# Filling TensorE's idle time with matmuls on zeros, an earlier load, sectioned norm columns and fewer table loads in a planned attention and channel-mix kernel

## The chip, the cores and the metric

The kernel runs on one core of one Trainium2 chip. The metric is the device time of one execution in microseconds (us), given as the median of several runs. "Span" is the time from the first to the last instruction in the trace; the device time is about 2 us longer.

Engines in the profile: PE is TensorE's matmul side, PEld its weight load, DVE is VectorE, ACT is ScalarE, POOL is GpSimd, SP is SyncE. L482 means line 482 of the kernel in question. The change shifts line numbers, so each matmul has a pair of them:

| work on TensorE | before | after |
|---|---|---|
| kv = kᵀv of a batch | L308 | L343 |
| transposes of q | L338 | L373 |
| u = q·kv | L358 | L393 |
| sum of squares for the norm | L383 | L425 |
| 1/rms spread to the rows ("rr") | L407 | L452 |
| w_k, w_r, w_v products of the mix | L482, L505, L524 | L537, L560, L580 |
| matmuls on zeros | none | L609 |

## The reference, cut to what matters

Batch 8, 8 heads, sequence 576, head dimension 64; d_model 512, d_ff 1024.

```python
def _attn_ref(q, k, v, g_norm):
    kv = np.einsum('bhsd,bhse->bhde', k, v)
    out = np.einsum('bhsd,bhde->bhse', q, kv)
    rms = np.sqrt(np.mean(out * out, axis=-1, keepdims=True) + 1e-06)
    return (out / rms * g_norm).astype(np.float32)

def _moe_ref(x, mu_k, mu_r, w_k, w_v, w_r):       # x: heads side by side, (8, 576, 512)
    x_prev = ...                                  # x shifted by one token, zeros first
    xk = mu_k * x + (1.0 - mu_k) * x_prev
    xr = mu_r * x + (1.0 - mu_r) * x_prev
    k = np.maximum(xk @ w_k, 0.0)
    v = k * k @ w_v
    r = 1.0 / (1.0 + np.exp(-(xr @ w_r)))
    return (r * v).astype(np.float32)
```

## The kernel before

The 8 batches of attention feed 9 groups of 512 tokens of the mix. Each group takes 32 w_k matmuls, 16 w_r matmuls and 32 w_v matmuls of 512 columns (in one group the w_k matmuls are 64 of 256 columns). All pieces of work are given to a planner in Python, which puts them in an order for each engine from durations it assumes, while the kernel is built. On the chip each engine then works through its own queue in that order: **a piece that waits holds up every piece behind it.** The timelines below show it: while one product of TensorE waits 6.74 us, nothing that stands behind it runs.

```python
class Planner:
    STAY, SWITCH = 4.0, 0.11        # only TensorE has a cost for changing the kind of work
    ...
    def run(self):
        ...                         # for each engine: of the pieces that can start within
        ...                         # 0.02 us of the earliest, the one with the smallest due
```

A piece names engines with assumed durations, the pieces it depends on, the buffers it uses, and `due`, its priority: the smaller, the sooner. This is how q gets transposed and when kv of a batch may start:

```python
        mm = add({"PE": 0.25 * n}, kv_mm, mode=1, bufs=[pkv, kin, vin, kv], due=due(26),
                 deps=[loaded[(m, b, h)] for m in ("k", "v") for h in (2 * hp0, 2 * (hp0 + n) - 1)])
        ...
        if b >= 2:
            def q_dma(_):
                nc.sync.dma_start_transpose(...)          # by DMA, from SyncE's queue
            m = add({"SP": 0.1}, q_dma, bufs=[qin, qT], due=due(30), deps=[loaded[("q", b, 0)]], land=4.2)
        else:
            for hp in hps:
                ...                                       # six transposes on TensorE, then a copy
```

The norm loads ScalarE's table for ln and exp each time, and works on few rows of many columns for the three small parts of batch 0:

```python
        def st_act(_):
            rows = slice(32 * hp0, 32 * hp0 + 32 * n)
            nc.scalar.preload_act_table_set("natural_log_exp_and_others")
            nc.scalar.activation(out=get(ln)[rows], in_=pst.t[rows, :, 0:HS], func=AF.Ln, bias=eps[rows],
                                 scale=1.0 / HD)
            nc.scalar.activation(out=get(rs)[rows], in_=ln.t[rows], func=AF.Exp, scale=-0.5)
```

The PSUM tiles "mm" (the mix) and "at" (attention) are rings of two each.

## Time and profile before

| | before |
|---|---|
| device time, median of 3 | 247.25 us (246.87 to 248.08) |
| span of the profiled run | 244.7 us |
| TensorE busy | 82% |
| first mix matmul | 24.3 us |
| end of TensorE's work | 240.4 us |

How to read it: the page's second part gives the busy share in tenths in 40 equal slices (6.1 us each), the row PEclk gives TensorE's granted clock in tenths of full speed, and the fourth part is the chain of work that ended last, followed back from the end. From the page of the kernel before:

```profile
PE 201.5 (82%) x1442; PEld 94.7 (39%) x1442; DVE 150.5 (62%) x273; ACT 114.4 (47%) x144; POOL 25.2 (10%) x39
...
PE   0564798961681997997999999799999999999981
...
PEclk9999999995586799999999999999999999999998
...
PE 54%; ACT 17%; DMA 17%; DVE 7%; issue 2%; POOL 1%; DVEq 0%; ACTq 0%; POOLq 0%
PE mm L524 22%; PE mm L482 17%; DMA qT<-q 14%; PE mm L505 9%; ACT L388 4%; ACT relu L486 3%; DMA v<-in_v_dram 3%; ACT ln L389 2%; DVE out L528 2%; ACT kv L184 2%; PE at L407 2%; ACT sig L509 2%; PE at L358 2%; ACT L509 2%; ACT rs L391 1%
```

The chain does not go to TensorE alone: the transposes of q by DMA hold 14% of the span. The PE row shows the hole, four slices at 1, 6, 8 and 1 tenths (55 to 80 us), where the clock is down as well (5, 5, 8 and 6). The busy time of the engines in a stretch (start:end and length; then busy time and instructions of PE, PEld, DVE, ACT and POOL; granted clock; DMA share; GB/s) of the kernel before:

```profile
55.00:81.00 26.00, 12.12 (x105) 5.25 (x101) 11.50 (x22) 9.39 (x14) 3.08 (x4) 0.63 1.17 189
```

In 26 us TensorE was busy for 12 us, at 0.63 of the clock. TensorE's timeline (start, duration, line, tile, count; in brackets the idle time before and what ended it) of the kernel before:

```profile
27.30 4.89 PE L505 MATMUL mm<-w_r,xr 128*128 128x512 bf16 x13 [0.17 <-DVE xr L445]
...
62.91 0.69 PE L358 MATMUL at<-qT,kv 64*64 64x288 bf16 x8 [6.74 <-DMA qT<-q]
...
65.03 3.60 PE L482 MATMUL mm<-xk,w_k 128*128 128x512 bf16 x8
...
78.91 0.46 PE L358 MATMUL at<-qT,kv 64*64 64x288 bf16 x4 [6.29 <-DMA qT<-q]
...
234.87 3.61 PE L524 MATMUL mm<-w_v,sqk 128*128 128x512 bf16 x16 [0.84 <-DVE out L528]
239.32 1.02 PE L524 MATMUL mm<-w_v,sqk 128*128 128x512 bf16 x4 [0.84 <-DVE out L528]
```

Two waits for a transposed q, 6.74 and 6.29 us, and after each a cold restart, which means matmuls at half the clock: after the first, 8 matmuls in 3.60 us are 0.45 us each, while 16 in 3.61 us (the line at 234.87) are 0.22 each; after the second (not shown) 4 take 1.70 us by the chain. The line at 27.30 is cold too (13 in 4.89 us, 0.376 each), though the clock row shows full rate there: the trace's own records of the clock begin only at 31.22 us, with a change to full, and the row has nines for all the time before. SyncE's timeline of the kernel before, one line for each group of issues:

```profile
44.66 7.17 SPq L327 DMA_TRANSPOSE qT<-q  x1
...
63.65 27.04 SPq L327 DMA_TRANSPOSE qT<-q  x3
```

The chain puts 18.2 us from the first issue, at 44.66, to its landing at 62.9, and 15.2 us for the next. Last, ScalarE's timeline of the kernel before at the start, the load and the ln of the second of three rounds of table load, ln and exp:

```profile
18.18 1.28 ACT L388 ACT_TABLE_LOAD   x1
19.48 0.73 ACT L389 ACTIVATE ln<-at,eps 32x576 f32<-32x576 f32 x1
```

### The profile page before, as it was taken

Reading aid. Unit: us, or ns where it says so; the run is one execution under the profiler, and the core shown is the slowest. Engines: PE = TensorE matmul, PEld = TensorE weight load, DVE = VectorE, ACT = ScalarE, POOL = GpSimd, SP = SyncE. Lnnn points to the kernel's source line nnn. Section 1 sums busy time; section 2 is a strip of 40 time slices with the busy share of each in tenths; the row PEclk is TensorE's granted clock in tenths of the full one; section 3 lists DMA queues with packets and bytes.
Section 4 is the critical chain, followed back from the end, with each engine's and each line's share of the span. In section 5 each row is a group of like instructions: output and inputs, shape, how many; then the busy total and the mean of one; then the engine's idle time right before and its main releaser. Section 6 shows DMA issues by size and latency. Waiting matters only on the chain.

```text
span 244.7 us, 3619 instructions
## 1 busy us (share of the span) xinstructions
PE 201.5 (82%) x1442; PEld 94.7 (39%) x1442; DVE 150.5 (62%) x273; ACT 114.4 (47%) x144; POOL 25.2 (10%) x39
## 2 busy tenths in 40 slices
PE   0564798961681997997999999799999999999981
PEld 0431245431230453443444457343444444444430
DVE  2359815857430898997899696589779323324222
ACT  2289257432371298089067426906731522513600
POOL 8860003302100124000000000000000000000000
PEclk9999999995586799999999999999999999999998
DMA  6999999999998969999074032004203205006023
GB/s 84 180 210 207 204 203 204 203 191 164 276 192 127 170 115 160 204 239 235 22 164 107 0 98 76 0 0 120 55 0 102 74 0 165 6 7 167 0 86 86
DMA packets 40832, 29.99 MB, mean 123 GB/s; under 512 B 15720, under 2 KB 35696, under 8 KB 40816
## 3 DMA queue, kind: packets, MB, share of 16 engines
q0 software_dynamic: 21008, 16.78, 44.6%
q1 hardware_dynamic: 19808, 12.99, 23.0%
q8 instruction: 11, 0.18, 0.3%
q14 instruction: 5, 0.04, 0.1%
HBM read 33.56 MB, written 9.44 MB: 176 GB/s over the span
## 4 chain that ended last, share of the span: by engine, by line
PE 54%; ACT 17%; DMA 17%; DVE 7%; issue 2%; POOL 1%; DVEq 0%; ACTq 0%; POOLq 0%
PE mm L524 22%; PE mm L482 17%; DMA qT<-q 14%; PE mm L505 9%; ACT L388 4%; ACT relu L486 3%; DMA v<-in_v_dram 3%; ACT ln L389 2%; DVE out L528 2%; ACT kv L184 2%; PE at L407 2%; ACT sig L509 2%; PE at L358 2%; ACT L509 2%; ACT rs L391 1%
## 5 line engine op out<-in xcount | busy, mean ns | idle before, releaser
L482 PE MATMUL mm<-xk,w_k 128*128 128x512 bf16 (+1 forms) x320 | 69.0, 368 | 0.7 <-ACT relu L486 0.4
L524 PE MATMUL mm<-w_v,sqk 128*128 128x512 bf16 x288 | 65.6, 379 | 3.6 <-DVE out L528 1.7
L486 ACT ACTIVATE relu<-mm 128x1024 bf16<-128x1024 f32 x36 | 36.5, 1021 | 50.6 <-PE mm L482 47.9
L482 PEld LDWEIGHTS <-w_k 128*128 128x128 bf16 x320 | 30.6, 99 | 31.9 <-issue 5.3
L524 PEld LDWEIGHTS <-sqk 128*128 128x128 bf16 x288 | 27.8, 98 | 35.8 <-issue 5.4
L528 DVE TENSOR_TENSOR out<-mm,sig 128x1024 f32<-128x1024 f32 (+1 forms) x20 | 22.3, 1116 | 26.2 <-PE mm L524 19.7
L489 DVE TENSOR_TENSOR sqk<-relu 128x1024 bf16<-128x1024 bf16 x36 | 24.5, 689 | 22.5 <-ACT relu L486 22.4
L505 PE MATMUL mm<-w_r,xr 128*128 128x512 bf16 x144 | 35.8, 400 | 1.4 <-DVE xr L445 1.4
L184 ACT CAST uT<-at 128x576 bf16<-128x576 f32 x18 | 11.2, 639 | 37.4 <-PE at L358 37.4
L414 DVE TENSOR_TENSOR xT<-uT,at 128x576 bf16<-128x576 bf16 (+1 forms) x31 | 21.7, 730 | 8.3 <-PE at L407 8.3
L509 ACT ACTIVATE sig<-mm 128x1024 bf16<-128x1024 f32 x18 | 18.2, 1025 | 10.7 <-PE mm L505 10.4
L505 PEld LDWEIGHTS <-xr 128*128 128x128 bf16 x144 | 14.1, 102 | 20.8 <-DVE xr L445 3.2
L441 DVE TENSOR_SCALAR t<-d,mu_sb 128x576 bf16<-128x576 bf16 x64 | 20.1, 372 | 0.1
L358 PE MATMUL at<-qT,kv 64*64 64x288 bf16 x116 | 8.4, 328 | 13.6 <-DMA qT<-q 13.0
L186 DVE CAST uT<-at 128x576 bf16<-128x576 f32 x11 | 8.3, 755 | 14.4 <-PE at L358 14.4
L367 DVE TENSOR_TENSOR sq<-uT 128x576 bf16<-128x576 bf16 x32 | 13.7, 453 | 4.5 <-ACT uT L184 4.2
L407 PE MATMUL at<-rs,selg 128*128 128x288 bf16 (+2 forms) x60 | 12.6, 306 | 4.8 <-DVE xT L414 1.8
L388 ACT ACT_TABLE_LOAD x10 | 12.8, 1283 | 0.2
L407 PEld LDWEIGHTS <-selg 128*128 128x128 bf16 (+2 forms) x64 | 6.1, 102 | 15.4 <-issue 11.1
L358 PEld LDWEIGHTS <-kv 64*64 64x64 bf16 x128 | 3.4, 111 | 22.3 <-issue 14.4
L247 POOL DMA_DIRECT2D k<-in_k_dram x10 | 7.5, 750 | 43.5 <-PE at L308 42.2
L184 ACT CAST kv<-at 64x256 bf16<-64x256 f32 x22 | 8.1, 368 | 8.3 <-PE at L308 5.1
(49 smaller groups left out, 127.6 us busy)
## 6 DMA issues: line engine op xcount, KB each, us to landing
out_dram<-out SPq DMA_DIRECT2D x24, 192.0 KB
k<-in_k_dram POOLq DMA_DIRECT2D x7, 576.0 KB, 12.4
v<-in_v_dram POOLq DMA_DIRECT2D x7, 576.0 KB, 17.2
q<-in_q_dram POOLq DMA_DIRECT2D x7, 576.0 KB, 17.4
out_dram<-out SPq DMA_DIRECT2D x24, 128.0 KB
out_dram<-out SPq DMA_DIRECT2D x24, 64.0 KB
w_k<-in_moe_w_k_dram POOLq DMA_DIRECT2D x1, 1024.0 KB, 12.6
w_v<-in_moe_w_v_dram POOLq DMA_DIRECT2D x1, 1024.0 KB, 16.7
```

Of the source, the lines that this page charges most:

```text
L184: nc.scalar.copy(out=dst, in_=src)
L388: nc.scalar.preload_act_table_set("natural_log_exp_and_others")
L407: nc.tensor.matmul(get(ps)[:, i, 0:HS], selg[rows, hp1 + i, :], rs.t[rows, half, :], start=True, stop=True)
L414: nc.vector.tensor_mul(out=xT.t[:, hs, xs], in0=get(uT)[:, hs].rearrange("q h i jj p -> q h (i jj p)")[:, :, cs], in1=ps.t[:, 0:step, 0:HS])
L441: nc.vector.tensor_scalar_mul(out=get(t)[:, hp - hp0, :], in0=d.t[:, hp, :], scalar1=mu_sb[:, m + hp:m + hp + 1])
L482: nc.tensor.matmul(get(ps)[:, fc % 2, a0:a1], w_k_sb[:, cc, 128 * fc:128 * fc + 128], xk[:, cc, x0:x0 + a1 - a0], start=(cc == 0), stop=(c ...
L486: nc.scalar.activation(out=get(rt), in_=ps.t, func=AF.Relu)
L489: nc.vector.tensor_mul(out=get(sqk)[:, 2 * f2:2 * f2 + 2, :], in0=rt.t, in1=rt.t)
L505: nc.tensor.matmul(get(ps)[:, ci % 2, :], xr[:, cc, n0:n0 + 128], w_r_sb[:, cc, :], start=(cc == 0), stop=(cc == NHP - 1))
L509: nc.scalar.activation(out=get(sg), in_=ps.t, func=AF.Sigmoid)
L524: nc.tensor.matmul(get(ps)[:, ci % 2, :], sqk.t[:, fc, 128 * ci:128 * ci + 128], w_v_sb[:, fc, :], start=(fc == 0), stop=(fc == NFC - 1))
L528: nc.vector.tensor_mul(out=get(ot)[:, xs, :], in0=ps.t[:, xs, :], in1=sg.t[:, xs, :])
```

## The change

Its announced intent has four parts: idle matmuls on zeros fill TensorE's gaps ahead of the mix, so that its clock is up when the mix starts; batch 1 loads ahead of w_v; the norm's columns are cut into sections that sit on more rows; a table is loaded only when it changes. The diff holds more than that: q of batch 2 is transposed on TensorE too (`b >= 3`), a rule keeps kv and q transposes of a batch behind the norm broadcast of the batch before (`last_rr`), there is a fourth output buffer, rings give any free slot, and ScalarE may scale by mu. The core of it:

```diff
 class Planner:
-    STAY, SWITCH = 4.0, 0.11
+    SWITCH = {"PE": 0.11, "ACT": 1.28}
+    SHUN = {"DVE": 0.5}
+    STAY = {"PE": 4.0, "ACT": 4.0}
 ...
+            if warm and p.eng == "PE":
+                since, until, idle = warm
+                n = int((t - max(free.get("PE", 0.0), since)) / 0.23)
+                if n > 0:
+                    order.append(lambda n=n: idle(n))
+                if p is until:
+                    warm = None
 ...
-        "out": (3, (128, 2, C), FP32),
+        "out": (4, (128, 2, C), FP32),
 ...
+    def ln_table():
+        if table[0] != "ln":
+            nc.scalar.preload_act_table_set("natural_log_exp_and_others")
+            table[0] = "ln"
 ...
-    p_wv = add({"POOL": 0.8}, lambda _: load_w(w_v_sb, moe_w_v), due=-698, land=5.2)
-    for b in range(1, B):
+    for n in ("k", "v", "q"):
+        load(1, n, 0, H, -698)
+    p_wv = add({"POOL": 0.8}, lambda _: load_w(w_v_sb, moe_w_v), due=-697, land=5.2)
+    for b in range(2, B):
 ...
-                 deps=[loaded[...] ...])
+                 deps=[loaded[...] ...] + [last_rr[b - 1]])          # kv; q's transposes likewise
 ...
-        if b >= 2:
+        if b >= 3:
 ...
-            m = add({"SP": 0.1}, q_dma, ..., land=4.2)
+            m = add({"SP": 3.2}, q_dma, ..., land=2.5)
 ...
         def st_act(_):
-            rows = slice(32 * hp0, 32 * hp0 + 32 * n)
-            nc.scalar.preload_act_table_set("natural_log_exp_and_others")
-            nc.scalar.activation(out=get(ln)[rows], in_=pst.t[rows, :, 0:HS], ...)
+            ln_table()
+            nc.scalar.activation(out=get(ln)[:, 0:wide, 0:w], in_=pst.t[:, 0:wide, 0:w], ...)
 ...
-            sc = add({"DVE": 0.25 * n}, ...)
+            sc = add({"DVE": 0.365 * n, "ACT": 0.7 * n}, ...)
 ...
+    def idle(n):
+        for _ in range(n):
+            nc.tensor.matmul(get(warm)[:, 0, :], zeros[:, 0:128], zeros, start=True, stop=True)
```

More of the change, by code (lines that the diff above doesn't have):

```diff
@@ L42, in __init__, with add @@
         self.left = []
-    def add(self, on, fn, deps=(), bufs=(), due=0.0, land=0.0, mode=0):
+    def add(self, on, fn, deps=(), bufs=(), due=0.0, land=0.0, mode=None):
         p = Piece(on, fn, deps, bufs, due, land, mode)
@@ L47, in add, with slots @@
         return p
+    def slots(self, tag):
+        out = []
+        for i, old in enumerate(self.rings[tag]):
+            if old is None:
+                out.append((0.0, i))
+            elif all(u.end is not None for u in old.users):
+                out.append((max(u.end for u in old.users) + 0.15, i))
+        return sorted(out)
     def room(self, bufs):
@@ L55, in room, with run @@
         for tag, bs in want.items():
-            for old in self.rings[tag][:len(bs)]:
-                if old is None:
-                    continue
-                if any(u.end is None for u in old.users):
-                    return None
-                t = max([t] + [u.end + 0.15 for u in old.users])
-        return t
-    def run(self):
-        free, order, dma, mode = {}, [], 0.0, 0
+            free = self.slots(tag)
+            if len(free) < len(bs):
+                return None
+            t = max(t, free[len(bs) - 1][0])
+        return t
+    def run(self, warm=None):
+        free, order, dma, modes = {}, [], 0.0, {"PE": None, "ACT": None}
         while self.left:
@@ L78, in run @@
                         t = max(t, d.end + (self.LAT[d.eng] if d.eng != eng or d.land else 0.0))
-                    ways.append((t + us, t, eng))
+                    ways.append((t + us + self.SHUN.get(eng, 0.0), t, eng))
                 _, t, eng = min(ways)
-                stay = self.STAY if eng == "PE" and p.mode == mode else 0.0
+                stay = self.STAY.get(eng, 0.0) if p.mode == modes.get(eng) else 0.0
                 best.setdefault(eng, []).append((t, p.due - stay, p))
@@ L87, in run @@
             t, _, p, p.eng = min(picks, key=lambda x: x[0])
+            if warm and p.eng == "PE":
[5 more added lines that the diff above has]
+                    warm = None
             p.start, p.end = t, t + p.on[p.eng]
-            if p.eng == "PE":
-                p.end += self.SWITCH * (p.mode != mode)
-                mode = p.mode
+            if p.eng in self.SWITCH and p.mode is not None or p.eng == "PE":
+                p.end += self.SWITCH[p.eng] * (p.mode != modes[p.eng])
+                modes[p.eng] = p.mode
             free[p.eng] = p.end
@@ L104, in run @@
                     b.placed = True
-                    self.rings[b.tag].append(b)
-                    self.rings[b.tag].pop(0)
+                    self.rings[b.tag][self.slots(b.tag)[0][1]] = b
             self.left.remove(p)
@@ L109, in run @@
         for p in order:
-            p.fn(p.eng)
-        return order
+            if isinstance(p, Piece):
+                p.fn(p.eng)
+            else:
+                p()
+        return [p for p in order if isinstance(p, Piece)]
 @with_exitstack
@@ L186, in copy @@
             nc.vector.tensor_copy(out=dst, in_=src)
+    table = [None]
+    def ln_table():
+        if table[0] != "ln":
+            nc.scalar.preload_act_table_set("natural_log_exp_and_others")
+            table[0] = "ln"
     ident = const.tile([128, 128], BF16, name="ident")
@@ L194 @@
     eps = const.tile([128, 1], FP32, name="eps")
+    zeros = const.tile([128, 512], BF16, name="zeros")
     sel2 = const.tile([128, 32], BF16, name="sel2")
@@ L204, in consts_small @@
     def consts_small(_):
+        nc.vector.memset(zeros, 0.0)
         nc.vector.memset(g_st, 0.0)
@@ L217, in consts_small @@
             nc.vector.memset(sel2[64 * e:64 * e + 64, e:e + 1], 1.0)
-        nc.scalar.preload_act_table_set("natural_log_exp_and_others")
+        ln_table()
     def consts_idents(_):
         make_identity(nc, ident)
-    p_mu_ps = Buf("at")
+    p_mu_ps, warm = Buf("at"), Buf("mm")
     def consts_mu(_):
@@ L236, in load_w @@
         nc.gpsimd.dma_start(out=dst, in_=src.rearrange("(c p) n -> p c n", p=128))
-    add({"DVE": 0.6}, consts_small, due=-1000)
+    add({"DVE": 0.9}, consts_small, due=-1000)
     src = {"k": k, "v": v, "q": q}
@@ L272 @@
     x_ready = {}
+    last_rr = {-1: None, 0: None}
     def attention(b, parts):
-        bufs = {t: Buf(t) for t in ("qT", "kv", "uT", "sq", "ln", "rs", "xT", "d")}
+        bufs = {t: Buf(t) for t in ("qT", "kv", "uT", "sq", "xT", "d")}
         x_ready[b] = {"k": [], "r": []}
@@ L291, in attention_part @@
         kin, vin, qin = (kvq[(m, b)] for m in ("k", "v", "q"))
-        kv, qT, uT, sq, ln, rs, xT, d = (bufs[t] for t in ("kv", "qT", "uT", "sq", "ln", "rs", "xT", "d"))
+        kv, qT, uT, sq, xT, d = (bufs[t] for t in ("kv", "qT", "uT", "sq", "xT", "d"))
+        ln, rs = Buf("ln"), Buf("rs")
         def due(x):
@@ L318, in attention_part @@
         mm = add({"PE": 0.25 * n}, kv_mm, mode=1, bufs=[pkv, kin, vin, kv], due=due(26),
-                 deps=[loaded[(m, b, h)] for m in ("k", "v") for h in (2 * hp0, 2 * (hp0 + n) - 1)])
+                 deps=[loaded[(m, b, h)] for m in ("k", "v") for h in (2 * hp0, 2 * (hp0 + n) - 1)] + [last_rr[b - 1]])
         kvs = [add({"DVE": 0.25 + 0.14 * n, "ACT": 0.38 + 0.11 * n}, lambda eng, e=e: kv_copy(eng, e), deps=[mm],
@@ L328, in q_dma @@
                     "q (y p) -> q y p", p=NP), in_=qin.t.rearrange("p h x -> p (h x)"))
-            m = add({"SP": 0.1}, q_dma, bufs=[qin, qT], due=due(30), deps=[loaded[("q", b, 0)]], land=4.2)
+            m = add({"SP": 3.2}, q_dma, bufs=[qin, qT], due=due(30), deps=[loaded[("q", b, 0)]], land=2.5)
             qts = {hp: m for hp in hps}
@@ L345, in attention_part @@
                 m = add({"PE": 0.35}, lambda _, hp=hp, ps=ps: q_tr(_, hp, ps), bufs=[ps, qin, qT], due=due(27),
-                        deps=[p_ident, loaded[("q", b, 2 * hp)], loaded[("q", b, 2 * hp + 1)]])
+                        deps=[p_ident, loaded[("q", b, 2 * hp)], loaded[("q", b, 2 * hp + 1)], last_rr[b - 1]])
                 qts[hp] = add({"ACT": 0.65, "DVE": 0.75}, lambda eng, hp=hp, ps=ps: q_cp(eng, hp, ps), deps=[m],
@@ L375, in attention_part @@
                            due=due(20)))
+        nsec = NHP // n
+        sec = S // nsec
         pst = ps_buf()
+        wide = 2 if sec > 512 else 1
+        w = sec // wide
         def st_mm(_):
-            for half in range(2):
-                for hp in hps:
-                    nc.tensor.matmul(get(pst)[32 * hp:32 * hp + 32, half, 0:HS], sel2,
-                                     sq.t[:, hp, HS * half:HS * half + HS], start=True, stop=True)
+            for x in range(wide):
+                for i, hp in enumerate(hps):
+                    for c in range(nsec):
+                        row = 32 * (i * nsec + c)
+                        nc.tensor.matmul(get(pst)[row:row + 32, x, 0:w], sel2,
+                                         sq.t[:, hp, sec * c + w * x:sec * c + w * x + w], start=True, stop=True)
         def st_act(_):
-            rows = slice(32 * hp0, 32 * hp0 + 32 * n)
-            nc.scalar.preload_act_table_set("natural_log_exp_and_others")
-            nc.scalar.activation(out=get(ln)[rows], in_=pst.t[rows, :, 0:HS], func=AF.Ln, bias=eps[rows],
+            ln_table()
+            nc.scalar.activation(out=get(ln)[:, 0:wide, 0:w], in_=pst.t[:, 0:wide, 0:w], func=AF.Ln, bias=eps,
                                  scale=1.0 / HD)
-            nc.scalar.activation(out=get(rs)[rows], in_=ln.t[rows], func=AF.Exp, scale=-0.5)
+            nc.scalar.activation(out=get(rs)[:, 0:wide, 0:w], in_=ln.t[:, 0:wide, 0:w], func=AF.Exp, scale=-0.5)
         m = add({"PE": 0.3}, st_mm, mode=2, deps=sqs, bufs=[pst, sq, ln, rs], due=due(18))
-        st = add({"ACT": 3.9 if b else 1.35}, st_act, deps=[m], bufs=[pst, ln, rs], due=due(17))
+        st = add({"ACT": 0.42 + 0.0018 * sec}, st_act, deps=[m], bufs=[pst, ln, rs], due=due(17), mode="ln")
         xms = []
@@ L404, in rr_mm @@
                 def rr_mm(_, hp1, half, ps):
-                    rows = slice(32 * hp0, 32 * hp0 + 32 * n)
                     for i in range(step):
-                        nc.tensor.matmul(get(ps)[:, i, 0:HS], selg[rows, hp1 + i, :], rs.t[rows, half, :],
-                                         start=True, stop=True)
+                        c0 = HS * half
+                        while c0 < HS * half + HS:
+                            c, off = divmod(c0, sec)
+                            x, off = divmod(off, w)
+                            cnt = min(HS * half + HS - c0, w - off)
+                            nc.tensor.matmul(get(ps)[:, i, c0 - HS * half:c0 - HS * half + cnt],
+                                             selg[:, (hp1 - hp0 + i) * nsec + c, :], rs.t[:, x, off:off + cnt],
+                                             start=True, stop=True)
+                            c0 += cnt
                 def x_mul(_, hp1, cs, xs, ps):
@@ L418, in attention_part @@
                 ps = ps_buf()
-                m = add({"PE": 0.26}, lambda _, hp1=hp1, half=half, ps=ps: rr_mm(_, hp1, half, ps),
+                m = add({"PE": 0.13 * step}, lambda _, hp1=hp1, half=half, ps=ps: rr_mm(_, hp1, half, ps),
                         deps=[st, p_mu], bufs=[ps, rs, xT], due=due(14))
-                xms.append(add({"DVE": 0.14 + 0.3 * step},
+                xms.append(add({"DVE": 0.15 + 0.3 * step},
                                lambda _, hp1=hp1, cs=cs, xs=xs, ps=ps: x_mul(_, hp1, cs, xs, ps),
                                deps=[m] + [us[hp1 + i] for i in range(step)], bufs=[ps, uT, xT], due=due(13)))
+        last_rr[b] = m
         def diff(eng):
@@ L437, in attention_part, with scale @@
             t = Buf("t")
-            def scale(_, m, t):
+            def scale(eng, m, t):
                 for hp in hps:
-                    nc.vector.tensor_scalar_mul(out=get(t)[:, hp - hp0, :], in0=d.t[:, hp, :],
-                                                scalar1=mu_sb[:, m + hp:m + hp + 1])
+                    dst, by = get(t)[:, hp - hp0, :], mu_sb[:, m + hp:m + hp + 1]
+                    if eng == "DVE":
+                        nc.vector.tensor_scalar_mul(out=dst, in0=d.t[:, hp, :], scalar1=by)
+                    else:
+                        nc.scalar.mul(out=dst, in_=d.t[:, hp, :], mul=by)
             def blend(_, dst, t):
@@ L448, in attention_part @@
             late = due(10 - 4 * pos) + (50 * pos if b == 0 else 0)
-            sc = add({"DVE": 0.25 * n}, lambda _, m=m, t=t: scale(_, m, t), deps=[df, p_mu], bufs=[d, t], due=late)
+            sc = add({"DVE": 0.365 * n, "ACT": 0.7 * n}, lambda eng, m=m, t=t: scale(eng, m, t), deps=[df, p_mu], bufs=[d, t], due=late)
             x_ready[b][key].append(add({"DVE": 0.06 + 0.34 * n}, lambda _, dst=dst, t=t: blend(_, dst, t), deps=[sc],
@@ L466, in store @@
             row += cnt
+    p_first = add({"PE": 0.01}, lambda _: None, deps=x_ready[0]["r"] + [p_wr], bufs=[warm], due=-1)
+    hold = add({"PE": 0.01}, lambda _: None, bufs=[warm], due=-2000)
     def mix(g):
@@ L508, in r_sig @@
         def r_sig(_, ps, sg):
+            table[0] = "sigmoid"
             nc.scalar.activation(out=get(sg), in_=ps.t, func=AF.Sigmoid)
@@ L516, in mix @@
                 ms.append(add({"PE": 0.865}, lambda _, ci=2 * c2 + x, ps=ps: r_mm(_, ci, ps),
-                              deps=ms or need["r"] + [p_wr], bufs=[ps, sg], due=u + x))
+                              deps=ms or need["r"] + [p_first], bufs=[ps, sg], due=u + x))
             sigs.append((sg, add({"ACT": 1.04}, lambda _, ps=ps, sg=sg: r_sig(_, ps, sg), deps=ms[1:], bufs=[ps, sg],
-                                 due=u + 2)))
+                                 due=u + 2, mode="sigmoid")))
         def v_mm(_, ci, part, ps):
@@ L548 @@
         mix(g)
-    plan.run()
+    def idle(n):
+        for _ in range(n):
+            nc.tensor.matmul(get(warm)[:, 0, :], zeros[:, 0:128], zeros, start=True, stop=True)
+    plan.run((1.5, p_first, idle))
 _INS = ['q', 'k', 'v', 'g_norm', 'moe_mu_k', 'moe_mu_r', 'moe_w_k', 'moe_w_v', 'moe_w_r']
```

## The prediction

> **What bounds the kernel now.** The 720 channel-mix matmuls of 512 columns take 6.91 us per 32 in the undisturbed late stretch (timeline), 155 us in all; attention of batches 1 to 7 adds about 3.3 us each on TensorE, with 1.4 us more where q is transposed there: about 181 us together. The mix starts at 24.3 us and TensorE ends at 240.4 us, 216 us. So about 35 us of that phase is not work. By the windows view:
> - 54.8 to 80.7 us: TensorE waits for the DMA transposes of q of batches 2 and 3. The chain of waits gives "DMA qT<-q" 14% of the span (18.2 and 15.2 us). The first was issued at 44.66 us behind queued loads of about 2.9 us each. TensorE then restarts at half clock (0.45 us per matmul instead of 0.216). The Trainium skill, "TensorE: Matmul & The Clock Gate", Part 1, says that an idle window of about 3.4 us halves the clock; the trace agrees (granted 0.50 to 0.59 after 6.7 us idle).
> - At 27.3 us, 13 matmuls take 4.89 us (0.376 each): cold too, about 2 us lost, although the clock row shows full rate.
> - Later iterations lose 1 to 1.5 us each around table loads and sigmoid; the end loses about 2 us to an output tile waiting for its store (three buffers).
>
> **What changes.** 64 zero matmuls go in ahead of the mix; k, v, q of batch 1 load before w_v; batch 2 is also transposed on TensorE, leaving 5 DMA transposes; table loads fall from 17 to 12 (1.28 us each; three of those removed are in the start-up chain); ln/exp of the first parts shrink from 576 columns (0.74 and 0.68 us) to 288 and 144 (I estimate 0.45 and 0.35); half of the mu scalings move to ScalarE (0.64 us each against 0.30 on VectorE); a fourth output buffer.
>
> **Costed on the critical path.**
> 1. Start: the ScalarE chain gets about 5 us shorter, but the zeros are unconditional and stand behind the mu matmul, which ends at 4.85 us: 18 of them at 0.43 us cold reach 11 to 12 us, while batch 0's first kv matmul ran at 7.7 us. I expect the first mix matmul at 27 to 29 us, but warm. Net near 0 to -2 us.
> 2. Batch 2's transpose wait disappears. Batch 3's is issued near 53 us and should land about when needed (wait 0 to 4 us). With the cold clock: -16 us.
> 3. New wait: group 1's w_k matmuls are now ordered ahead of group 0's w_v ones, so TensorE waits for xk of batch 1, behind busy ScalarE and VectorE: about 42 to 51 us, +6 us net.
> 4. Steady iterations: r matmuls, then ln, exp, table load and sigmoid on ScalarE: about 1.5 us of wait each, as before: 0 to +2.
> 5. End: -2 us.
>
> Sum: 181 us of work, start at 28, 18 us of waits, tail 4.3: span about 231, time 2.3 more.
>
> **Prediction: 233 us, 224 to 241 (8 in 10). Faster by over 2%: 0.88; within 2%: 0.09; slower: 0.03.**
>
> **Right or wrong in the profile.** The chain's share of "DMA qT<-q" under 3%; clock row full from 30 us on, or one dip at 42 to 51 us; first real w_r matmul between 27 and 29 us; first w_v matmul after 50 us; no output wait for a store at the end.
>
> **What would make it wrong.** If the zeros don't delay the start (mix by 24 us) and the wait for xk is short: 224. If batch 3's and 4's transposes still land late, or a cold restart follows at 45 us: 240.

## More of the kernel before

The mix, for group g (`slot = 20 * g`); relu is on ScalarE, its square on VectorE, and the first w_v matmul of a group needs all four squares:

```python
            a = add({"ACT": 1.04}, ..k_relu.., deps=ms[1:], bufs=[ps, rt], due=u + 2)
            sqs.append(add({"DVE": 0.7}, ..k_sq.., deps=[a], bufs=[rt, sqk], due=u + 4))
        ...
        for c2 in range(2):
            ps, ot, u = Buf("mm"), Buf("out"), slot + 12 + 4 * c2
            ...                                   # w_v matmuls, deps on sqs
```

## The result, and the profile after

Ratios are the mean time of one kernel's runs over that of the other's runs of the same rounds, so they are not quite the ratio of the medians quoted. Executions over 1.5% slower than the fastest of the same kernel are left out of the means.

| | before | after |
|---|---|---|
| device time, median of 4 | 247.06 us (246.62 to 248.08) | 239.5 us (238.14 to 239.78) |
| ratio to before, 95% interval | | 0.9677 (0.9636 to 0.9718) |
| span of the profiled run | 244.7 us | 236.1 us |
| TensorE busy | 82% | 91% |
| first mix matmul | 24.3 us | 28.05 us |
| end of TensorE's work | 240.4 us | 231.7 us |
| table loads | 17 | 12 |

The kernel is 3.2% faster; 5.7% was predicted. The profiled run of after is the fastest of its runs, the others have spans of 237.1 to 237.8 us. From the page of after:

```profile
PE 214.8 (91%) x1538; PEld 100.4 (43%) x1538; DVE 137.3 (58%) x233; ACT 136.1 (58%) x184; POOL 25.2 (11%) x39
...
PE   2988999579987999989998998999899999999971
...
PEclk9999999857997999999999999999999999999997
...
PE 79%; DVE 10%; ACT 6%; issue 2%; POOL 1%; DVEq 0%; POOLq 0%
PE mm L537 27%; PE mm L580 25%; PE mm L560 12%; DVE xT L461 5%; PE mm L609 5%; PE at L393 3%; PE at L452 2%; PE at L343 2%; DVE out L584 2%; ACT t L493 1%; DVE d L478 1%; PE at L425 1%; ACT ln L430 1%; PE at L373 1%; ACT kv L205 1%
```

No transpose of q stands in the chain any more, and TensorE has 79% of it. Of TensorE's 214.8 us busy, 18.0 us are the matmuls on zeros (by the lines view), so the rise from 82% to 91% is for the most part the fillers. The clock row has two dips instead of one. The same stretches as windows of after:

```profile
40.30:58.60 18.30, 14.26 (x124) 7.14 (x121) 13.41 (x25) 12.50 (x18) 2.48 (x3) 0.72 1.29 194
...
69.80:76.00 6.20, 4.38 (x29) 1.54 (x32) 5.79 (x9) 4.37 (x7) 1.90 (x3) 0.75 1.28 220
76.00:231.70 155.70, 150.29 (x977) 70.06 (x976) 88.69 (x130) 91.57 (x113) 3.83 (x5) 1.00 0.47 92
```

TensorE's timeline of after, with the lines that answer those of before:

```profile
4.77 5.67 PE L609 MATMUL mm<-zeros 128*128 128x512 bf16 x18
10.37 0.57 PE L343 MATMUL mm<-v,k 96*64 96x64 bf16 x24
...
24.39 3.83 PE L609 MATMUL mm<-zeros 128*128 128x512 bf16 x17
28.05 1.03 PE L560 MATMUL mm<-w_r,xr 128*128 128x512 bf16 x4
...
33.01 0.42 PE L373 MATMUL at<-ident,q 96*128 96x96 bf16 x6
...
43.93 0.65 PE L452 MATMUL at<-rs,selg 128*128 128x288 bf16 x4 [1.69 <-ACT rs L432]
...
46.51 0.64 PE L373 MATMUL at<-ident,q 96*128 96x96 bf16 x6
...
53.31 1.89 PE L537 MATMUL mm<-xk,w_k 128*128 128x512 bf16 x4
...
58.62 1.03 PE L580 MATMUL mm<-w_v,sqk 128*128 128x512 bf16 x4
...
71.04 0.32 PE L393 MATMUL at<-qT,kv 64*64 64x288 bf16 x4 [0.83 <-DVE uT L207]
72.23 0.32 PE L393 MATMUL at<-qT,kv 64*64 64x288 bf16 x4 [0.87 <-ACT uT L205]
72.67 3.36 PE L537 MATMUL mm<-xk,w_k 128*128 128x512 bf16 x8
...
226.22 3.61 PE L580 MATMUL mm<-w_v,sqk 128*128 128x512 bf16 x16 [0.84 <-DVE out L584]
```

Four readings:

- The 18 zero matmuls at 4.77 us take 5.67 us. At the warm rate of 0.216 us each they would take 3.9, so some of them ran at half clock: by the trace's single records the first eight start 0.43 us apart, 3.4 us in all, and the rest 0.216 (the Trainium skill, "TensorE: Matmul & The Clock Gate", Part 1, calls the warm-up a budget of about 3.4 us of time, not a number of matmuls, and this fits). The fillers stand ahead of the first kv matmul, which comes at 10.37 us; before it came at 7.7 us. The mix starts at 28.05, 3.7 us later than before, but warm.
- From 40.3 to 58.6 us TensorE waits in pieces: for exp of batch 1's norm at 43.93, then (lines not shown) for VectorE and ScalarE piece by piece until the first w_k matmuls of group 1 at 53.31. The first w_v matmul of group 0 is planned behind all of that, at 58.62; before, group 0's w_v began at 42.2 us, by the chain. The work in this stretch is 24 w_k matmuls at 0.216 us, 5.2 us, and 3.8 us of attention pieces of batches 1 and 2 at the warm durations that the same pieces have elsewhere in this trace: about 9.0 us. So 9.3 us are lost, to waits and to a clock of 0.72 that makes the work itself longer.
- From 69.8 to 76.0 us there are 2.7 us of work, so 3.5 us are lost. The w_k matmuls at 72.67 run at 0.42 us each: the clock fell to half at 72.9 us, though no wait shown ahead of it is longer than 0.87 us; TensorE had been busy for 1.2 of the last 3 us. Such waits do not always cool it (see a_no_zeros). In the traces the clock changes only at times a multiple of 3.41 us apart (in after at 45.61, 55.85, 72.92 and 76.33), so it may depend on where the waits fall on that grid; this is argued, not tested.
- The wait of 0.84 us ahead of the block at 226.22 stays, as does the one after it (the same 0.84 us, not shown).

SyncE's timeline of after, where the first transpose (now batch 3) is issued, and VectorE's at the second dip:

```profile
53.44 11.96 SPq L362 DMA_TRANSPOSE qT<-q  x2
```

```profile
70.24 0.75 DVE L207 CAST uT<-at 128x576 bf16<-128x576 f32 x1
...
71.40 1.22 DVE L584 TENSOR_TENSOR out<-mm,sig 128x1024 f32<-128x1024 f32 x1
```

The first u product that needs the DMA's transpose runs at 69.8 us without waiting for it. In the dip that follows, VectorE has a uT copy, a square (not shown) and the out product of group 0 (L584) in its queue, and the PSUM tile that the next w_k pair wants is free only when that out product ends, at 72.6 us. Two lines of ScalarE's timeline of after show the norm in sections, ln on 128 rows of 288 and of 144 columns instead of 576 columns:

```profile
17.68 0.50 ACT L430 ACTIVATE ln<-at,eps 128x288 f32<-128x288 f32 x1
...
20.88 0.38 ACT L430 ACTIVATE ln<-at,eps 128x144 f32<-128x144 f32 x1
```

### The profile page after: what moved, and what is told of

Its sections match the earlier page's. It is cut to its first block, busy times and chain, and to the rows that moved or that the text cites. A ratio compares the mean times of both kernels' runs of the same rounds, so it can differ in the third digit from the quotient of the medians.

```text
span 236.1 us, 3800 instructions
## 1 busy us (share of the span) xinstructions
PE 214.8 (91%) x1538; PEld 100.4 (43%) x1538; DVE 137.3 (58%) x233; ACT 136.1 (58%) x184; POOL 25.2 (11%) x39
## 4 chain that ended last, share of the span: by engine, by line
PE 79%; DVE 10%; ACT 6%; issue 2%; POOL 1%; DVEq 0%; POOLq 0%
PE mm L537 27%; PE mm L580 25%; PE mm L560 12%; DVE xT L461 5%; PE mm L609 5%; PE at L393 3%; PE at L452 2%; PE at L343 2%; DVE out L584 2%; ACT t L493 1%; DVE d L478 1%; PE at L425 1%; ACT ln L430 1%; PE at L373 1%; ACT kv L205 1%
## 5 line engine op out<-in xcount | busy, mean ns | idle before, releaser
L580 PE MATMUL mm<-w_v,sqk 128*128 128x512 bf16 x288 | 65.5, 379 | 2.0 <-DVE out L584 1.7
L584 DVE TENSOR_TENSOR out<-mm,sig 128x1024 f32<-128x1024 f32 (+1 forms) x20 | 22.3, 1116 | 25.0 <-PE mm L580 24.9
L560 PE MATMUL mm<-w_r,xr 128*128 128x512 bf16 x144 | 32.9, 380 | 0.0
L493 ACT ACTIVATE t<-d,mu_sb 128x576 bf16<-128x576 bf16 x34 | 23.7, 764 | 4.0 <-DVE d L478 2.4
L205 ACT CAST uT<-at 128x576 bf16<-128x576 f32 x23 | 13.9, 641 | 10.0 <-PE at L393 10.0
L609 PE MATMUL mm<-zeros 128*128 128x512 bf16 x64 | 18.0, 410 | 0.0
L452 PE MATMUL at<-rs,selg 128*128 128x288 bf16 (+1 forms) x62 | 11.1, 285 | 6.1 <-DVE xT L461 4.3
L205 ACT CAST kv<-at 64x256 bf16<-64x256 f32 x24 | 8.8, 366 | 12.9 <-PE at L343 12.5
L278 POOL DMA_DIRECT2D q<-in_q_dram x10 | 7.5, 751 | 48.5 <-DMA qT<-q 31.4
L452 PEld LDWEIGHTS <-selg 128*128 128x128 bf16 x68 | 6.5, 97 | 12.9 <-issue 10.3
L496 DVE TENSOR_TENSOR xk<-t,xT 128x2304 bf16<-128x2304 bf16 (+2 forms) x10 | 11.2, 1116 | 0.5 <-ACT t L493 0.4
L478 DVE TENSOR_TENSOR d<-xT 128x2304 bf16<-128x2304 bf16 (+2 forms) x10 | 11.2, 1119 | 0.3
```

Of the source, the lines that this page charges most:

```text
L205: nc.scalar.copy(out=dst, in_=src)
L452: nc.tensor.matmul(get(ps)[:, i, c0 - HS * half:c0 - HS * half + cnt], selg[:, (hp1 - hp0 + i) * nsec + c, :], rs.t[:, x, off:off + cnt], ...
L493: nc.scalar.mul(out=dst, in_=d.t[:, hp, :], mul=by)
L560: nc.tensor.matmul(get(ps)[:, ci % 2, :], xr[:, cc, n0:n0 + 128], w_r_sb[:, cc, :], start=(cc == 0), stop=(cc == NHP - 1))
L580: nc.tensor.matmul(get(ps)[:, ci % 2, :], sqk.t[:, fc, 128 * ci:128 * ci + 128], w_v_sb[:, fc, :], start=(fc == 0), stop=(fc == NFC - 1))
L584: nc.vector.tensor_mul(out=get(ot)[:, xs, :], in0=ps.t[:, xs, :], in1=sg.t[:, xs, :])
```

## The experiments

**The theory to be tested.** The announced parts net to little. What pays is that no transpose of q by DMA is waited for; part of the gain is lost again because group 0's w_v products are planned behind batch 1's attention chain. **The rivals.** The gain is the warm clock at the start; or the load order; or the shorter norm chain and the saved table loads. In the texts the theories carry letters, A and on, and each text says what a letter expects there.

Sizes below are differences of ratios times 247.3 us. Where a variant is compared with after, the two ratios come from different batches, each against the kernel before on its own chip, so such a size is good to about 1 us. The medians of before were 247.67, 247.30 and 247.78 us in the three batches. There is a second caution: 3.4 us at half clock cost 1.7 us, and the second dip of after (72.9 to 76.3 us) is absent from the profiled executions of a_no_zeros and a_wide_norm, so a small shift can bring or spare it. Sizes of 1 to 2 us can be of that origin. In the names, "a" is an edit of the kernel after and "b" of the kernel before.

### a_no_zeros: no matmuls on zeros

```diff
     def idle(n):
-        for _ in range(n):
-            nc.tensor.matmul(get(warm)[:, 0, :], zeros[:, 0:128], zeros, start=True, stop=True)
+        pass
```

> The changed kernel without its 64 zero matmuls, all else in the same order. Theory A (the fillers buy next to nothing, because v and q of batch 1 land only at about 28 and 31 us and the ScalarE chain behind them sets the pace): batch 0's first kv matmul goes back to about 7.7 us, the first w_r matmul comes at 24 to 26 us and cold, TensorE then waits for v of batch 1; the time stays within 1.5 us of the changed kernel, ratio to before 0.962 to 0.974. Rival B (the warm clock is a main source of the gain): at least 2.5 us slower than the changed kernel, ratio 0.978 or more.

Measured: 239.76 us (238.04 to 240.25, 6 runs), ratio 0.968 (0.9651 to 0.9709). That is after's own ratio. TensorE's timeline of this variant:

```profile
24.02 0.61 PE L560 MATMUL mm<-w_r,xr 128*128 128x512 bf16 x1 [3.06 <-DVE xr L496]
...
27.86 1.50 PE L343 MATMUL at<-v,k 96*64 96x64 bf16 x48 [1.81 <-DMA v<-in_v_dram]
...
75.65 1.89 PE L537 MATMUL mm<-xk,w_k 128*128 128x512 bf16 x8 [0.65 <-DVE out L584]
```

The mix starts 4 us sooner, cold, and by 27.86 it waits for a load of batch 1. So the 64 fillers, as they are placed, are worth nothing in the total. The trace shows that they do gain at first: without them the w_k matmuls begin 1.0 us later than in after (34.26 against 33.27, not shown) and group 0's w_v 2.5 us later (61.08 against 58.62). Without them, though, the waits for uT near 74 us (1.35, 0.35 and 0.65 us) did not cool TensorE: the 8 w_k matmuls at 75.65 run warm, where after's at 72.67 are cold. That the total is zero rests in part on this dip, which the fillers were not meant to touch.

### a_zeros_early: the first block of zeros ahead of the mu matmul

```diff
+        first = next(x for x in order if not isinstance(x, Piece))   # the first block of fillers
+        order.remove(first)
+        order.insert(order.index(self.before), first)                # self.before = p_mu
         for p in order:
```

> The changed kernel with its first 18 zero matmuls issued ahead of the mu matmul, so that they start at about 1.5 us instead of 4.8 us. Theory A: batch 0's first kv matmul at about 8 us instead of 10.4, but the batch 1 loads land as before, so at most 1 us gained (ratio 0.962 to 0.969). Rival B' (the late start is what the fillers cost): 2 to 3 us gained, ratio about 0.957.

Measured: 237.48 us (237.0 to 237.89, 4 runs), ratio 0.9595 (0.957 to 0.962), 2.0 us faster than after. TensorE's timeline of this variant (its line numbers are 4 higher):

```profile
1.19 5.62 PE L613 MATMUL mm<-zeros 128*128 128x512 bf16 x18 [1.19 <-DVE zeros L238]
...
7.93 0.57 PE L347 MATMUL mm<-v,k 96*64 96x64 bf16 x24 [0.81 <-DMA v<-in_v_dram]
...
25.72 1.03 PE L564 MATMUL mm<-w_r,xr 128*128 128x512 bf16 x4
```

The same 18 fillers now run while TensorE has nothing to do, the first kv matmul is back at 7.93 us, and the mix starts at 25.72 us, warm. I had expected at most 1 us; the rival in the text was nearer. The fillers do help, if they don't stand ahead of real work.

### b_q2_pe: in the kernel before, q of batch 2 transposed on TensorE, and nothing else

```diff
-        if b >= 2:
+        if b >= 3:
```

> The kernel before with one part of the change alone: q of batch 2 is transposed on TensorE. Theory A (the wait for the DMA transposes is where the gain comes from): 6 to 10 us faster than before, ratio 0.960 to 0.976, with some wait left for batch 3's transpose; DMA qT share of the chain falls from 14% to below 5%. Rival C (the other parts make the gain): ratio 0.985 or more.

Measured: 245.72 us (245.25 to 246.06, 4 runs), ratio 0.9923 (0.9893 to 0.9952). Only 2 us; theory A's 6 to 10 us were missed. TensorE's timeline of this variant:

```profile
63.08 1.49 PE L308 MATMUL at<-v,k 96*64 96x64 bf16 x48 [3.17 <-DMA v<-in_v_dram]
...
75.01 0.46 PE L358 MATMUL at<-qT,kv 64*64 64x288 bf16 x4 [5.85 <-DMA qT<-q]
```

One wait is replaced by another: the planner now has kv of batch 4 ahead in TensorE's queue, which waits for its load, and later u of batch 3 waits 5.85 us for its transpose. So moving the transpose alone does not explain the gain.

### a_sqk0: group 0's relu and squares first

```diff
-            a = add({"ACT": 1.04}, ..k_relu.., due=u + 2)
-            sqs.append(add({"DVE": 0.7}, ..k_sq.., due=u + 4))
+            a = add({"ACT": 1.04}, ..k_relu.., due=u + 2 - 40 * (g == 0))
+            sqs.append(add({"DVE": 0.7}, ..k_sq.., due=u + 4 - 40 * (g == 0)))
```

> The changed kernel with the relu and squares of group 0 ahead of attention of batch 1 on ScalarE and VectorE, so that group 0's w_v matmuls are ready while xk of batch 1 is still being made. Theory A (the order is what cost the missing 3%): the w_v matmuls start at 43 to 45 us, TensorE's wait at 42 to 58 us falls from 9 to under 4 us, no second cold stretch at 70 to 76 us; 5 to 8 us faster than the changed kernel, ratio 0.935 to 0.949. Rival D (ScalarE and VectorE are simply full between 40 and 60 us, so what is moved ahead delays attention by as much): within 1.5 us of the changed kernel.

Measured: 235.44 us (234.96 to 238.11, 4 runs; the profiled one is the slow end of them), ratio 0.9536 (0.9492 to 0.958), 3.5 us faster than after, less than the 5 to 8 expected. TensorE's timeline of this variant:

```profile
42.98 3.02 PE L580 MATMUL mm<-w_v,sqk 128*128 128x512 bf16 x11
...
90.91 0.32 PE L393 MATMUL at<-qT,kv 64*64 64x288 bf16 x4 [1.19 <-DVE uT L207]
...
94.34 3.59 PE L560 MATMUL mm<-w_r,xr 128*128 128x512 bf16 x8
```

Group 0's w_v now starts at 42.98 us instead of 58.62, the dip at 40 to 58 us is gone (clock 1.00 in that stretch), but a wait of the same kind comes at 89 to 94 us, where TensorE waits for VectorE's and ScalarE's copies of uT and restarts cold (8 in 3.59 us), and again near 112 us (not shown). So in this order the wait at 40 to 58 us has the cause I gave it, and a part of it moves on. How much is not shown: the profiled execution is the slowest, at a mean clock of 0.976, and the other three, 2.7 us faster and more at 0.986 to 0.993, must have been cold for less time.

### b_q2_order: the kernel before with both the q transposes of batch 2 and the order rule

```diff
-        if b >= 2:
+        if b >= 3:
 ...
-                 deps=[loaded[...] ...])                        # kv; q's transposes likewise
+                 deps=[loaded[...] ...] + [last_rr[b - 1]])
 ...
+        last_rr[b] = m                                          # the last norm broadcast of batch b
```

> The kernel before with two parts of the change: q of batch 2 on TensorE, and the rule that no kv product or TensorE transpose of batch b is planned ahead of batch b-1's norm products. Nothing of the load order, the fillers, the sections or the tables. Theory F (formed after q on TensorE alone gave only 0.8%: TensorE's queue runs in order, so any piece of a later batch that is planned too early exposes TensorE to a late load, and both parts are needed): 7 to 11 us faster than before, ratio 0.955 to 0.972, no wait over 1 us for a load of v or k after 40 us. Rival G (the gain lies in the start, the load order or ScalarE): ratio 0.985 or more.

Measured: 240.18 us (239.43 to 243.14, 4 runs; the 243.14 is not in the ratio), ratio 0.9704 (0.9648 to 0.976). These two small parts, neither of them announced, give 7.3 us, nearly all that the whole change gives (8.0 by its ratio). Theory F holds. The rule alone adds 5.4 us to the 2 us of b_q2_pe; without the transposes it was not run. No wait for a load or a DMA transpose is left in TensorE's timeline after 40 us. Group 0's w_v begins at 41.04 us, ahead of group 1's w_k, so the order that step 3 of the prediction is about does not occur here; even so there are waits for VectorE (1.50 us at 51.5, 0.90 at 57.8) and a stretch at half clock from 53.5 to 63.8 us.

### a_q2_dma: after with q of batch 2 by DMA again

```diff
-        if b >= 3:
+        if b >= 2:
```

> The changed kernel with q of batch 2 transposed by the DMA again. Theory F: the transpose is issued when q of batch 2 has landed, at about 44 us, with loads of batches 3 and 4 queued, and lands at 57 us or later; TensorE waits for it 4 us or more, and the kernel is 4 to 10 us slower than the changed one, ratio 0.984 to 1.01. Rival G: within 1.5 us of the changed kernel.

Measured: 248.3 us (247.44 to 249.68, 4 runs), ratio 1.0041 (0.9995 to 1.0086). Taking this one line back costs 9.0 us and leaves nothing of the gain. TensorE's timeline of this variant:

```profile
63.35 0.69 PE L393 MATMUL at<-qT,kv 64*64 64x288 bf16 x8 [7.71 <-DMA qT<-q]
```

The wait for the transpose, 7.71 us, is back.

### a_wv_first: after with w_v loaded ahead of batch 1 again

```diff
-        load(1, n, 0, H, -698)
+        load(1, n, 0, H, -696)
```

> The changed kernel with w_v loaded ahead of batch 1 again. Theory H (the load order brings nothing by itself: batch 1's attention comes 5 us later, but group 0's w_v matmuls fill TensorE in the meantime): within 2 us of the changed kernel, ratio 0.960 to 0.976, and the bubble at 42 to 53 us shrinks. Rival I (the load order is a source of the gain): 2.5 us or more slower, ratio 0.978 or more.

Measured: 239.08 us (237.8 to 239.28, 4 runs), ratio 0.9652 (0.9612 to 0.9691), the same as after within the intervals. Theory H holds: the load order brings nothing by itself. TensorE's timeline of this variant:

```profile
43.29 1.04 PE L580 MATMUL mm<-w_v,sqk 128*128 128x512 bf16 x4
```

Group 0's w_v comes ahead of group 1's w_k here, as in before, and most of the wait at 42 to 53 us is gone, as expected. But waits for copies of kv (1.14 and 0.76 us) and half clock follow at 57 to 65 us, and the time is after's. An early w_v alone does not bring the lost time back.

### a_table_each: after with a table load at every norm

```diff
         def st_act(_):
+            table[0] = None
             ln_table()
```

> The changed kernel with a table load ahead of every ln again, 17 loads instead of 12, instructions else in the same order. Theory J (in the start-up the first load lies on the chain, the later ones fall into ScalarE's gaps): the first w_r matmul comes 1.3 to 2.5 us later, the kernel is 1 to 3 us slower, ratio 0.972 to 0.980. Rival K (the fillers hold the start back anyway, so the saved loads bring nothing): within 0.7 us, ratio 0.965 to 0.971.

Measured: 243.49 us (242.14 to 244.45, 6 runs), ratio 0.9833 (0.9795 to 0.9871), 3.9 us slower than after. In this variant's trace the mix starts at 30.84 us, 2.8 us later than in after, and there is a wait of 0.87 us for exp at 65.5 us. The clock is at half from 24.6 to 28.0 us in this trace, which is part of the later start. TensorE also waits 1.69 us for a sigmoid at 84.9 us, where after waits 0.22 us. J's 1 to 3 us was too small, and K is refuted: saved table loads do count.

### a_wide_norm: after with the norm on few rows of 576 columns again

```diff
-            nc.scalar.activation(out=get(ln)[:, 0:wide, 0:w], in_=pst.t[:, 0:wide, 0:w], ...)
+            rows = slice(0, 32 * n)
+            nc.scalar.activation(out=get(ln)[rows], in_=pst.t[rows, :, 0:HS], ...)     # exp likewise,
 ...                                                    # and the matmuls around them as in before
```

> The changed kernel with the norm columns not in sections: ln and exp of the first parts run over 64 or 32 rows and 576 columns again, instead of 128 rows and 288 or 144 columns; order else the same. Worked out from the two traces: the first pair 0.48 us longer, the other two 0.72 us longer each, of which ScalarE's gaps (1.45 and 0.84 us before the second and third ln) take most: mix 0.5 to 1.2 us later, 0.5 to 1.2 us slower than the changed kernel, ratio 0.970 to 0.974. Rival: hidden altogether, within 0.3 us.

Measured: 240.28 us (239.99 to 242.01, 6 runs), ratio 0.972 (0.9686 to 0.9754). The sections are worth about 1.1 us, near the noise, although the mix starts at 30.36 us in this trace, 2.3 us later. So a part of an earlier start is taken back later: here the w_k matmuls at 75.91 us run warm (8 in 1.89 us, not shown), where after's at 72.67 are cold.

### a_tail: two PSUM tiles for the last pairs of the last group

```diff
-            ps, ot, u = Buf("mm"), Buf("out"), slot + 12 + 4 * c2
+            pss = (ps, ps) if g < NG - 1 else (ps, Buf("mm"))      # one tile for each half of a pair
 ...                                                                # matmuls and out use pss[x]
```

> The changed kernel with one mend, in the last group one PSUM tile for each half of an output pair, so that w_v matmuls of one half and the VectorE product of the other needn't wait for each other. The two waits of 0.84 us before the last w_v matmuls go: 1.4 to 1.8 us faster than the changed kernel, ratio 0.960 to 0.963. Rival (the wait is not of the shared tile): no change.

Measured: 236.89 us (236.1 to 237.76, 6 runs), ratio 0.9565 (0.9533 to 0.9596), 2.8 us faster than after. TensorE's timeline of this variant at the end:

```profile
222.66 7.07 PE L580 MATMUL mm<-w_v,sqk 128*128 128x512 bf16 x32
```

32 matmuls in one piece: both waits of 0.84 us, which before and after share, came from one PSUM tile holding two halves. The waits explain 1.7 us; the other 1 us is within what such a size is good for.

### a_best: zeros early, group 0's squares first, and the tail, together

The edits are those of a_zeros_early, a_sqk0 and a_tail.

> The changed kernel with three mends together: the first fillers ahead of the mu matmul (2 us faster alone), relu and squares of group 0 first (4 us alone), and in the last group one PSUM tile for each half of an output pair. If the three add up: 231 to 233.5 us, ratio 0.930 to 0.944, mix from about 25.7 us, no second wait at the end. If early start and reordered group 0 lean on the same loads and ScalarE chain, they don't add up: 234 to 235.5 us.

Measured: 234.5 us (231.36 to 234.8, 6 runs in two clusters), ratio 0.9435 (0.9389 to 0.9481), 6.0 us faster than after, where the three alone sum to 8.3. They add up in part. The profiled execution is one of the slower cluster (mean clock 0.973; the two fast ones 0.988 and 0.990), and its clock row still has dips at 87 to 99 and 110 to 116 us.

### a_best_all: the same, with relu and squares first in every group

```diff
-            ... due=u + 2 - 40 * (g == 0))
-            ... due=u + 4 - 40 * (g == 0)))
+            ... due=u + 2 - 40)
+            ... due=u + 4 - 40))
```

> As a_best, but relu and squares go first in all groups. In the order of the instructions the norm products of the later batches then stand between w_v and w_k matmuls instead of in one block behind w_r. If those blocks cost what the trace of the changed kernel shows (1.3 us each, four of them), 2 to 5 us faster than a_best. Rival: the ScalarE and VectorE time that attention loses comes back as waits for xk: within 1.5 us of a_best, or slower.

Measured: 224.96 us (224.41 to 225.01, 5 runs), ratio 0.9078 (0.9053 to 0.9102). This version beats both kernels: 9.2% faster than before, and 8.8 us faster than a_best by the ratios (9.5 by the medians), where 2 to 5 was expected. From the page of a_best_all:

```profile
PEclk9999999999999999999999999999999999999998
```

The clock never falls below nine tenths until the end. In its timeline the norm broadcasts (four matmuls, 0.5 us) stand between blocks of mix matmuls and no longer in a row, so that the waits for VectorE are covered by work: from 60 to 76 us, TensorE is busy for 15.86 of 16.0 us.

## Why the prediction was right or wrong

**Right.** The class, faster by over 2%, and the time lies in the predicted range, near its upper end. The prediction had named this case itself: "a cold restart follows at 45 us: 240"; in after's trace the clock falls to half at 45.6 us. Of its list for the profile all holds but the clock row, which has two dips and not one.

- *Step 1, the start.* "First mix matmul at 27 to 29 us, but warm. Net near 0 to -2 us": 28.05 us, warm, and a_no_zeros puts the net at 0.1 us. The Trainium skill, "TensorE: Matmul & The Clock Gate", Part 1, has an idle window of about 3.4 us behind the half clock; the trace agrees in kind, with restarts at 0.42 to 0.45 us per matmul after waits of 6.3 to 6.7 us.
- *Step 2, the transposes.* The chain's share of q's transposes went from 14% to none, and batch 3's was not waited for. The size of 16 us fits the hole: in 26 us before, TensorE was busy for 12. But the *reason* was incomplete. I credited it to moving batch 2's transposes; b_q2_pe shows 2 us for that alone. The order rule, which the prediction does not name, is needed with it. And as a saving 16 us was too much: b_q2_order gets 7.3 us from both together, with group 0's w_v ahead of group 1's w_k, and in its trace waits for VectorE and a cold stretch stand where the hole was. That the total still fell into the range is in part luck: the saved table loads, measured at 3.9 us, are in the prediction only within a start of 0 to -2 us.
- *Step 4, later groups.* 1.5 us each were predicted, for table loads and sigmoid on ScalarE. The total came out near, but not by that mechanism: from 76 us on TensorE is idle for 5.4 us, of which 0.22 are for a sigmoid, 1.7 are the two waits at the end, and the rest, 0.86 us in each of four groups, are norm broadcasts that wait for VectorE. The first two of them, in TensorE's timeline of after:

```profile
102.58 0.40 PE L452 MATMUL at<-rs,selg 128*128 128x288 bf16 x2 [0.60 <-DVE xT L461]
103.25 0.41 PE L452 MATMUL at<-rs,selg 128*128 128x288 bf16 x2 [0.26 <-DVE xT L461]
```

The step from a_best to a_best_all is 8.8 us and touches nothing but the order of relu and squares of groups 1 to 8.
- *Step 5, the end.* The wait for a store is gone; the two waits for a PSUM tile stay, as a_tail shows.

**Wrong: the size of step 3.** "TensorE waits for xk of batch 1 ... about 42 to 51 us, +6 us net." The mechanism was right (the first w_v matmul comes at 58.62, predicted after 50), but the term was too small. The stretch from 40.3 to 58.6 us lost 9.3 us, and a second stretch of the same origin, 69.8 to 76.0 us, lost another 3.5 us: 12.8 against 6. Two things were not in the 6: the clock falls with the waits (0.72 over the stretch), so the work in it takes longer too, which the prediction named only as what would make it wrong; and group 0's w_v, once late, puts its out product into VectorE's queue in the middle of batch 3's attention, where it holds the PSUM tile of the next w_k pair. a_sqk0 changes nothing but the order of group 0's relu and squares and gets 3.5 us of it back, and a_best_all, with relu and squares first everywhere, has no stretch at half clock left between 6.8 and 221.9 us. But the late w_v is not the whole cause: in a_wv_first and b_q2_order group 0's w_v is early (43.29 and 41.04 us), and neither is clearly faster than after. What all three timelines share is TensorE waiting for the attention of batches 1 and 2 on VectorE and ScalarE; that this is what costs the time is argued, not shown apart.

The sum: the mix starts at 28.05 and TensorE ends at 231.7 us, 203.7 us for 181 us of work, so 22.6 us of waiting or slow clock where 18 were predicted. Step 3 is 6.8 us over. That leaves 9.8 us for all else, where the prediction had 12; 5.4 of them are the idle time above, and the other 4.4 no idle time shows: the 181 us are themselves an estimate. The rest of the 6.5 us between 233 and 239.5 is mostly that the profiled run was 1.4 us faster than the median.

**Where the expected gain went.** The parts measured one by one are: q of batch 2 with the order rule 7.3 us, table loads 3.9, sections 1.1, load order 0, fillers 0. They sum to about 12 us, and the change gives 8.0. So the theory's "the announced parts net to little" fails for the table loads and holds for the other three. The difference is of the size that a_sqk0 brings back; that the late w_v of group 0 is what takes it is argued from the timeline and from that run, not shown: a_wv_first speaks against it as the only cause, and the parts do not add up linearly (a_best got 6.0 of 8.3).

**Open.** What the fourth output buffer and mu scaling on ScalarE are worth singly; what the order rule alone is worth, in before and in after; and why a_best's and a_sqk0's runs fall into clusters 2 to 3 us apart. The faster runs of both show a higher mean clock, so a cold stretch that comes in some executions only would fit, but only slower ones were profiled.

## What to carry to other kernels

In an engine that runs its queue in order, a piece of later work that stands too early exposes everything behind it to that piece's load or transpose: look at which piece of the queue waits, not only at what it waits for, and tie pieces to the stage before when their input may be late. Give the short operations that feed the big engine (here relu and square) priority over longer side work on the same engines, so that the big engine always has ready work; that was worth more here than all the announced parts. Work that only keeps a clock up must never stand ahead of real work.

## What the Trainium skill lacked or had wrong

- "TensorE: Matmul & The Clock Gate", Part 1: it does not say whether matmuls on zeros raise the clock. They do: with 18 fillers ahead of them the first 24 kv matmuls take 0.57 us (10.37 us in after), without fillers 0.85 us (7.55 us in a_no_zeros).
- The same page, Part 4, says that the full clock "doesn't engage" for transpose mode. Here `nc.tensor.transpose`, which the trace lists as a MATMUL with the identity, follows the clock: six of q take 0.42 us where it is up (33.01 us in after) and 0.64 us where it is at 0.50 (46.51 us). Whether transposes alone would raise the clock, no run here shows.
- "ScalarE: Activation LUTs", What ACT_TABLE_LOAD costs: it gives about 1283 ns and a drain of about 1380 ns more for a switch to another set. The load is 1.28 us here, but no drain shows: at a switch in before, exp ends at 113.09 us, the load runs from 113.11 to 114.39, and the sigmoid starts at 114.41.
- "DMA: Bandwidth & Descriptors", DMA Transpose (X-bar): its section on transposes says nothing of how long one takes beside queued loads. Here it took 18.2 and 15.2 us from issue to landing in before.
